# A written-out order for pooled attention and routed attention experts: another list of steps, PSUM banks and copy engines

## The chip, the core and the metric

The kernel runs on one core of a Trainium2 chip. A core has a matrix engine (TensorE, here PE), three elementwise engines (VectorE or DVE, ScalarE or ACT, GpSimd or POOL) and SyncE (SP), which here only issues stores. Each engine works through its own queue in order; engines wait for each other through semaphores. Matmul results go to PSUM, which has eight banks of 512 float32 columns in each of 128 partitions[...]. Times are microseconds (us) on the device; smaller is better.

## The reference

There are two parts. The first is attention with pooled keys and values: for each of 8 batches and 8 heads, 576 queries of 64 elements, and keys and values averaged over groups of 8 rows, so that 72 of each are left.

```python
k_p = k.reshape(B, H, Sp, pool, D).mean(axis=3)
v_p = v.reshape(B, H, Sp, pool, D).mean(axis=3)
scores = scale * np.matmul(q, k_p.transpose(0, 1, 3, 2))
attn = softmax(scores)                 # over the 72 pooled keys
x = np.matmul(attn, v_p)               # heads side by side: 576 x 512 per batch
```

The second takes that x. Four experts of width 64 each do causal attention over the 576 rows; a gate picks two experts for every row and weighs them.

```python
logits = x @ w_gate                    # top 2 of 4, softmax over the two
for e in range(E):
    q, k, v = x @ wq[e], x @ wk[e], x @ wv[e]
    a = softmax(causal(scale * q @ k.T))
    out += gate[e] * (a @ v @ wo[e])   # zero where e is not picked
```

## The kernel before

The work is cut into named steps, and a written-out list (`SEQ`, line 551) says in which order they are emitted. A token is a step, its arguments, the batch and, where it applies, the bank: `P_q1:0@7c` is the step P with arguments q and 1, of batch 0, into bank 7, cut into strips. The loop at line 642 reads the tokens one by one and calls the step's function. The framework turns data dependencies into semaphores; the order within PE, ACT, DVE and POOL is that of the list, and nothing else orders them. So a token's place in the list matters only against others of the same engine, and the relative place of tokens of two engines has no effect of its own.

**PE steps**, with their number over all batches:

- `PK`, `PV` (8 each) average k and v by a matmul with a constant matrix, into 32-column strips; `KT` (8) and `Q` (32) transpose the pooled k and the q.
- `E` (40) are the scores of two heads at once, each from 64 rows of the array; `E4` is the tail of 64 columns for all heads. `D` (24) sums the exponentials, `O` (40) multiplies them by pooled v, both in strips of 32 columns.
- `P` (40) projects x to the experts' q and k (`P_t` is the tail of 64 rows), `V` (36) to v and the gate's logits, in chunks of 128 rows.
- `S` (56) are the experts' scores, two experts at once from 64 rows each; `B` (36) multiplies their exponentials by v; `T` (24) transposes the result; `Y` (36) multiplies by wo.
- `H` are warm-up matmuls on zeros, 51 in all.

Three shapes of the array occur: whole (128 or 96 columns from over 64 rows), strips (32 columns) and half rows (64 rows). `PK`, `PV`, `D` and `O` are always in strips, `E` and `S` always in half rows. A trailing `c` on a token (`cut`, line 179) makes `wide` (line 187) cut a whole matmul into four strips of 32 columns with the same result.

**Reading steps** have small letters: each takes its PE step's bank out to SBUF. `e` and `s` (exponentials), `d` (logarithm of the sums) and `x` (exponential of its negative) are always ACT's; `o` and the normalisation `bz`, `bg`, `b` always DVE's; so are nine of the ten gate steps `g`. For `kc`, `kt`, `vc`, `r` (transposed q), `p`, `v`, `t` and `y` (the result), a trailing `d` chooses DVE, none ACT. `c0` to `c4` put the weights in order.

**POOL** issues every load: `L_q0:3` is the first of six loads of q for batch 3, `L_k` and `L_v` have three each, `W0` to `W4` load the weights, converting float32 to bfloat16 as they go. There are three raw buffers each for q, k and v (`NRAW`, line 55), so a load of batch b waits until batch b - 3 has been used. Between the loads POOL does the causal masks `a` (`am`, line 442): one instruction for each diagonal block of 128, two blocks for the tiles 1 and 2.

**Stores** are issued by SP as soon as a `y` is done (`z`, line 536); the last ones partly by ACT. Y4 of the last batch is cut into two halves of 256 columns in two banks, `ya` and `yb`.

Of the kernel before, what the change touches and what calls it, by code (L numbers as in the profile page):

```python
# [21 lines left out]
def kernel(  # L22
# [152 lines left out]
    def copy(dve, out, in_):  # L175
        (nc.vector.tensor_copy if dve else nc.scalar.copy)(out=out, in_=in_)  # L176
# [334 lines left out]
    def Y(b, bank, c):  # L511
        p0 = 128 * place(b, c)
        last = (b, c) == (B - 1, 4)
        for n0 in (0, 256) if last else (0,):
            n = 256 if last else 512
            for ep in range(NEP):
                wide(psum[:, bank ^ (n0 > 0), n0 : n0 + n],
                     oTs[2 * (b // 2 % 2) + ep][:, p0 : p0 + 128], wop[:, ep, n0 : n0 + n],
                     start=(ep == 0), stop=(ep == NEP - 1))

    def y(b, bank, dve, c, half=None, later=False):
        ofin = at[b, "ofin", c] if (b, "ofin", c) in at else ofp.tile([128, DM], FP32, name="ofin", tag="ofin")
# [13 lines left out]
    def z(b, c, queue):  # L536
# [15 lines left out]
        I:0 L_k0:0 L_k1:0 L_k2:0 J:0 K:0 H19:0@0 PK:0@0 kc:0 H4:0@1 KT:0@0 kt:0 L_q0:0 L_q1:0  # L552
        L_q2:0 L_q3:0 L_q4:0 L_q5:0 H8:0@1 Q2:0@0 r2:0 Q1:0@1 Q3:0@2 r1:0d r3:0 H1:0@3 E2:0@4
        e2:0 Q0:0@1 r0:0 E3:0@2 H5:0@0 E0:0@4 e3:0 L_v0:0 L_v1:0 E4:0@0 L_v2:0 PV:0@6 vc:0d e4:0
        e0:0 H2:0@2 D2:0@0 E1:0@2 O11:0@1 e1:0 H4:0@6 O01:0@2 O20:0@3 D1:0@4 d1:0 D0:0@5 x1:0
        M:0 L_k0:1 L_k1:1 L_k2:1 O10:0@6 O00:0@7 PK:1@4 d0:0 L_q0:1 o10:0 L_q1:1 L_q2:1 L_q3:1
        L_q4:1 kc:1d H3:0@5 KT:1@6 L_q5:1 H5:0@4 Q0:1@4 Q3:1@5 d2:0 x0:0 o01:0 o00:0 kt:1 o11:0
        x2:0 r0:1d W0:0 Q1:1@2 o20:0 W1:0 Q2:1@1 c0:0 E0:1@6 r3:1 r1:1d E3:1@4 c1:0d E1:1@2 e0:1
        c2:0d c3:0d P_q0:0@0 e3:1 W2:0 r2:1d W3:0 e1:1 P_t0:0@6 p_q0:0d p_t0:0d L_v0:1 P_k0:0@1
        S03:0@4 E4:1@6 E2:1@2 P_k1:0@0c c4:0d s03:0 L_v1:1 e4:1 V3:0@4c D2:1@5 D0:1@6 p_k1:0d  # L560
        p_k0:0d v3:0d P_q1:0@7c e2:1 D1:1@0 S00:0@2 d0:1 L_v2:1 d2:1 V1:0@6c p_q1:0d x0:1 s00:0
        V0:0@7c v0:0d PV:1@1 S01:0@2 S12:0@4 d1:1 V2:0@0c vc:1d x2:1 O20:1@1 v1:0d o20:1 s01:0
        O01:1@7 v2:0 L_k0:2 O11:1@6 x1:1 O00:1@2 L_k1:2 o01:1 o00:1 a03:0 O10:1@3 V4:1@0c o10:1
        o11:1 L_k2:2 s12:0 PK:2@1 P_t0:1@7 S02:0@4 kc:2 S10:0@2 g0:0 g1:0 v4:1 g2:0 KT:2@1
        L_q0:2 V3:1@6 V0:1@0 p_t0:1d s02:0 s10:0 g3:0 V2:1@7 kt:2d L_q1:2 L_q2:2 g4:0 L_q3:2
        L_q4:2 v3:1d L_q5:2 Q0:2@1 v2:1d Q3:2@6 v0:1 g5:0 r3:2d V1:1@2 Q1:2@0 Q2:2@3 r0:2 E0:2@6
        v1:1 E3:2@4 r1:2d a01:0 E1:2@0 e0:2 P_k0:1@2c g1:1 r2:2d P_q1:1@3c e1:2 g6:0 p_k0:1d
        e3:2 L_v0:2 L_v1:2 p_q1:1d D0:2@0 g0:1 L_v2:2 g7:0 g8:0 PV:2@1 vc:2d E2:2@6 d0:2 L_k0:3
        e2:2 E4:2@4 g2:1 P_q0:1@3c O00:2@2 L_k1:3 x0:2 O01:2@1 a00:0 O10:2@0 a10:0 L_k2:3 D1:2@6
        P_k1:1@7c e4:2 D2:2@4 d1:2 L_q0:3 x1:2 p_q0:1d d2:2 L_q1:3 a02:0 o01:2 O11:2@1 o00:2  # L570
        g3:1 PK:3@6 p_k1:1d L_q2:3 o11:2 S00:1@2 kc:3 S11:0@4 B01:0@7 L_q3:3 L_q4:3 o10:2 g4:1
        B00:0@6 g5:1 g6:1 g9:0 bz00:0 L_q5:3 KT:3@1 L_v0:3 P_q0:2@0 bz01:0 g7:1 kt:3d x2:2
        L_v1:3 g8:1 a12:0 g9:1 s11:0 L_v2:3 L_k0:4 p_q0:2d a11:0 V1:2@4 bg00:0 bg01:0 s00:1
        B10:0@5 v1:2 L_k1:4 S01:1@2 b00:0 S02:1@0 bz10:0 s01:1 L_k2:4 bg10:0 V0:2@4 L_q0:4
        L_q1:4 a01:1 B11:0@6 s02:1 b01:0 V3:2@7 Q1:3@2 v3:2 v0:2d Q2:3@4 b10:0 bz11:0 T0:0@5
        r1:3d S10:1@0 r2:3 bg11:0 E1:3@2 Q3:3@7 s10:1 b11:0 t0:0d r3:3d T1:0@6 Q0:3@5 P_k0:2@4
        S03:1@0 e1:3 t1:0d L_q2:4 L_q3:4 s03:1 L_q4:4 E3:3@6 r0:3d E4:3@2 e4:3 P_k1:2@5 L_q5:4
        p_k0:2d a00:1 p_k1:2d L_v0:4 E2:3@0 S12:1@2 PV:3@4 a03:1 e3:3 P_q1:2@5c vc:3d e2:3
        E0:3@0 s12:1 p_q1:2d W4:0 a02:1 L_v1:4 S11:1@6 B01:1@4 e0:3 bz01:1 bg01:1 B00:1@5 D1:3@2
        D2:3@3 O20:2@0 bz00:1 b01:1 o20:2 a12:1 s11:1 PK:4@1 D0:3@4 d1:3 d2:3 bg00:1 x1:3  # L580
        O00:3@6 L_v2:4 V2:2@0c O11:3@7 kc:4d O20:3@1 L_k0:5 b00:1 d0:3 o11:3 O10:3@3 v2:2 o10:3
        O01:3@2 Y3:0@5 a10:1 x0:3 P_t0:2@4 o01:3 Y1:0@0 x2:3 a11:1 o00:3 L_k1:5 B10:1@3 y3:0
        p_t0:2 Q0:4@2 y1:0 g1:2 o20:3 S01:2@4 S03:2@6 bz10:1 Y2:0@0c r0:4d s01:2 bg10:1 Y0:0@1c
        s03:2 PV:4@2 S02:2@4 b10:1 S12:2@6 y0:0d B11:1@3 g2:2 y2:0 vc:4d s02:2 Q1:4@0 Q2:4@1
        bz11:1 KT:4@2 Q3:4@4 T0:1@5 g3:2 r1:4d bg11:1 s12:2 kt:4d P_q0:3@0 b11:1 r3:4 r2:4d
        t0:1d E1:4@6 p_q0:3d e1:4 E3:4@2 E0:4@4 L_k2:5 P_k0:3@1 e3:4 T1:1@0 V2:3@6 P_q1:3@7
        E4:4@2 p_k0:3d g0:2 t1:1d g4:2 L_q0:5 L_q1:5 L_q2:5 v2:3d p_q1:3d e0:4 e4:4 S00:2@0
        E2:4@4 P_k1:3@6c e2:4 s00:2 Y3:1@7c L_q3:5 D0:4@2 L_q4:5 PK:5@3 D1:4@4 O11:4@5 y3:1d
        V1:3@7 p_k1:3d L_q5:5 d1:4 V0:3@0 Q3:5@4 kc:5 g5:2 L_v0:5 L_v1:5 v1:3d x1:4 KT:5@3 v0:3d
        Q0:5@7 P_t0:3@6 a12:2 Q1:5@0 r3:5d L_v2:5 d0:4 o11:4 r0:5d kt:5 Q2:5@1 S11:2@2 S10:2@4  # L590
        O00:4@7 p_t0:3 L_k0:6 x0:4 r1:5d O10:4@0 O01:4@6 L_k1:6 r2:5d s11:2 Y2:1@1c V4:3@2c
        o00:4 L_k2:6 L_q0:6 o01:4 s10:2 L_q1:6 a00:2 o10:4 D2:4@3 PV:5@7 Y0:1@6c y2:1 d2:4
        E4:5@4 vc:5 S00:3@0 L_q2:6 v4:3d y0:1d g6:2 a03:2 L_q3:6 L_q4:6 S02:3@2 x2:4 e4:5 V3:4@7
        g7:2 P_q0:4@6 L_q5:6 v3:4d s02:3 S10:3@4 p_q0:4d g8:2 s00:3 s10:3 S01:3@2 V3:3@7c L_v0:6
        v3:3d O20:4@6 P_k0:4@0c g1:3 o20:4 a11:2 s01:3 PK:6@1 p_k0:4d E1:5@4 g2:3 S11:3@6 e1:5
        E2:5@2 a01:2 a10:2 e2:5 P_k1:4@0 kc:6d g9:2 s11:3 B10:2@1 P_t0:4@4 Q3:6@5 V0:4@2 g3:3
        p_k1:4d L_v1:6 p_t0:4 bz10:2 L_v2:6 bg10:2 Y1:1@0 E3:5@6 a10:3 L_k0:7 g4:3 v0:4 r3:6d
        g0:3 E0:5@4 b10:2 y1:1 a02:2 S03:3@2 g5:3 B01:2@1 L_k1:7 B11:2@0 L_k2:7 s03:3 g6:3 a02:3
        B00:2@2 a00:3 g7:3 Q1:6@3 L_q0:7 e0:5 bz01:2 e3:5 KT:6@4 g8:3 g9:3 bz11:2 bg11:2 bg01:2
        V2:4@5 b11:2 L_q1:7 Q2:6@0 bz00:2 bg00:2 r1:6d b01:2 r2:6d D1:5@6 kt:6 D2:5@7 O10:5@4  # L600
        b00:2 a01:3 d1:5 d2:5 L_q2:7 v2:4d O01:5@3 x1:5 L_q3:7 x2:5 PV:6@1 D0:5@0 P_q1:4@7c
        O20:5@5 O00:5@2 vc:6d d0:5 a03:3 O11:5@6 x0:5 S12:3@0 o10:5 L_q4:7 T0:2@4 p_q1:4 a11:3
        o20:5 P_t0:5@5 o00:5 o01:5 s12:3 t0:2d p_t0:5 B01:3@7 B00:3@2 bz01:3 S02:4@0 o11:5
        L_q5:7 bg01:3 a12:3 bz00:3 s02:4 L_v0:7 E1:6@4 T1:2@3 B10:3@6 b01:3 V0:5@7 bg00:3 t1:2d
        bz10:3 V1:4@3 e1:6 bg10:3 v0:5 b00:3 S01:4@0 S00:4@4 b10:3 L_v1:7 Q0:6@2 v1:4d s01:4
        B11:3@6 Y0:2@3 P_k0:5@7 r0:6d bz11:3 E2:6@0 bg11:3 y0:2d S03:5@2 s00:4 b11:3 L_v2:7
        s03:5 E3:6@4 V1:5@6 p_k0:5d a02:4 T0:3@7 T1:3@2 v1:5d e2:6 e3:6 t0:3d Y1:2@3 P_q1:5@0
        S03:4@6 E0:6@4 t1:3d s03:4 y1:2d e0:6 g1:4 E4:6@2 e4:6 Y4:1@1c p_q1:5d a01:4 g2:4
        O11:6@6 D1:6@0 V2:5@7c D0:6@4 V3:5@5c D2:6@2 PK:7@3 y4:1d d1:6 g3:4 d2:6 x1:6 v3:5d kc:7
        O10:6@0 O01:6@1 g4:4 Y1:3@5c v2:5d o10:6 o11:6 P_k1:5@7c O00:6@0 d0:6 S10:4@2 y1:3  # L610
        p_k1:5d x0:6 S12:4@4 Q3:7@6 o01:6 s10:4 P_q0:5@7 KT:7@1 Q0:7@2 s12:4 V4:5@3 o00:6 kt:7
# [93 lines left out]
```

The softmax here doesn't subtract the row's maximum and nothing guards it: scores larger than these inputs give would overflow.

## Time and profile before

| | |
|---|---|
| median of 3 runs | 167.99 us |
| the runs | 167.83, 167.99, 222.52 us |
| span of the profiled execution | 165.0 us |
| its own time as a run | not given; the median is 3.0 us above the span |
| TensorE clock granted, mean | 0.996 |
| busy: PE, ACT, DVE, POOL | 157.0, 135.0, 123.8, 104.9 us |
| matmuls, and weight loads | 2463 each |
| last matmul starts, last copy ends | 160.37, 161.15 us |

A slice line of the page gives each engine's busy share in 40 equal slices of the span, in tenths; a timeline line gives start, length, engine, line, instruction, result and operands, shapes and count, and in brackets the idle time before it and what ended it. A group line gives, behind the bar, busy time and mean length. Matmuls overlap in the pipeline, so the time from one start to the next is what one costs. Most PE instructions have the line of the helpers `mm` (185) or `flip` (194) and most copies that of `copy` (176), so the tiles' names tell them apart: `qraw`, `kraw`, `vraw` are loads, `eta` the first part's exponentials, `xT` its transposed result, `qk` the experts' q and k, `etb` their exponentials, `vaug` their v, `osc` and `oT` the scaled result and its transpose, `ofin` the output.

### The profile page before, as it was taken

To read this page: it belongs to the slowest core of one execution; us is meant where nothing else is said; L and a number is where in the kernel's file an instruction comes from. 1 tells how busy PE (TensorE), PEld (TensorE's weight loads), DVE (VectorE), ACT (ScalarE), POOL (GpSimd) and SP (SyncE) were. 2 spreads that over 40 slices of the span, in tenths; PEclk is the share of its full clock that TensorE was granted. 3 is DMA by queue.
4 is the path that set the end of the run, shared out by engine and by line. 5 is a ranking of instruction groups with operands and counts; after the bars stand their busy time and mean duration, and the time that the engine had idled before them with its cause. 6 is when DMAs were issued, how large, how long until landed. Compare 5 with 4: busy or idle time off the path is not lost. (4 is left out here: it accounts for less than half of the span.)

```text
span 165.0 us, 6106 instructions
## 1 busy us (share of the span) xinstructions
PE 157.0 (95%) x2463; PEld 93.8 (57%) x2463; DVE 123.8 (75%) x410; ACT 135.0 (82%) x247; POOL 104.9 (64%) x178
## 2 busy tenths in 40 slices
PE   6999988999999999999999999999999999999980
PEld 2344354568557656654754878555647686555730
DVE  1101497589799859976988899998998989779960
ACT  3029758999998999888998997789997999898860
POOL 6999891899999999965959997400140211364100
PEclk9999999999999999999999999999999999999998
DMA  2999999999999999999999999923113043055875
GB/s 22 160 153 171 164 172 178 170 145 139 177 156 173 164 157 148 156 233 217 206 178 226 168 198 83 174 100 86 47 68 127 4 131 127 0 190 195 257 260 191
DMA packets 84204, 25.04 MB, mean 152 GB/s; under 512 B 79312, under 2 KB 79568, under 8 KB 84176
## 3 DMA queue, kind: packets, MB, share of 16 engines
q0 software_dynamic: 78928, 15.21, 110.6%
q1 hardware_dynamic: 5024, 9.05, 15.9%
q8 instruction: 19, 0.31, 0.7%
q10 hardware_dynamic: 224, 0.39, 0.6%
q14 instruction: 9, 0.07, 0.1%
HBM read 30.42 MB, written 9.44 MB: 242 GB/s over the span
## 5 line engine op out<-in xcount | busy, mean ns | idle before, releaser
L433 ACT ACTIVATE etb_97<-psum 128x1024 bf16<-128x1024 f32 x24 | 23.6, 1023 | 2.5 <-PE psum L185 2.4
L433 ACT ACTIVATE etb_98<-psum 128x1024 bf16<-128x1024 f32 x24 | 23.5, 1027 | 1.3 <-PE psum L185 1.1
L450 POOL TENSOR_SCALAR_AFFINE_SELECT etb_98<-etb_98 128x256 bf16<-128x256 bf16 x32 | 12.5, 410 | 17.4 <-ACT etb_98 L433 17.2
L450 POOL TENSOR_SCALAR_AFFINE_SELECT etb_97<-etb_97 128x256 bf16<-128x256 bf16 x32 | 12.4, 415 | 15.8 <-ACT etb_97 L433 15.7
L173 PE MATMUL psum<-warm 128*128 128x512 bf16 x51 | 15.2, 443 | 1.8 <-DVE onesd L146 1.3
L273 ACT ACTIVATE eta_91<-psum 96x1024 bf16<-96x1024 f32 x16 | 15.9, 1018 | 1.1 <-PE psum L185 1.1
L273 ACT ACTIVATE eta_92<-psum 96x1024 bf16<-96x1024 f32 x16 | 15.6, 1020 | 0.7 <-PE psum L185 0.6
L117 POOL DMA_DIRECT2D qraw_68<-in_q_dram x18 | 13.9, 775 | 1.2 <-PE psum L185 1.1
L176 DVE COPY ofin<-psum 128x512 f32<-128x512 f32 (+1 forms) x18 | 11.9, 673 | 3.2 <-PE psum L185 2.4
L117 POOL DMA_DIRECT2D qraw_69<-in_q_dram x18 | 13.8, 770 | 0.5 <-issue 0.5
L176 DVE CAST qk_99<-psum 128x512 bf16<-128x512 f32 (+1 forms) x16 | 10.5, 670 | 3.8 <-PE psum L185 3.6
L176 DVE CAST qk_100<-psum 128x512 bf16<-128x512 f32 (+1 forms) x16 | 10.5, 654 | 3.5 <-PE psum L185 3.5
L176 ACT COPY ofin<-psum 128x512 f32<-128x512 f32 (+1 forms) x19 | 10.7, 580 | 2.7 <-PE psum L185 1.8
L185 PE MATMUL psum<-wvg,xT_96 128*32 128x260 bf16 (+1 forms) x120 | 10.8, 275 | 0.0
L173 PEld LDWEIGHTS <-warm 128*128 128x128 bf16 x51 | 5.1, 111 | 9.5 <-issue 5.8
L185 PE MATMUL psum<-wvg,xT_95 128*32 128x260 bf16 (+1 forms) x156 | 10.5, 275 | 0.0
L185 PEld LDWEIGHTS <-etb_97 128*128 128x128 bf16 x240 | 8.8, 97 | 2.0 <-issue 0.4
L117 POOL DMA_DIRECT2D qraw_70<-in_q_dram x12 | 9.2, 784 | 0.0
L185 PEld LDWEIGHTS <-etb_98 128*128 128x128 bf16 x240 | 8.3, 97 | 1.4 <-issue 0.8
L185 PE MATMUL psum<-qk_100 64*128 64x64 bf16 (+4 forms) x96 | 8.8, 276 | 0.1
L117 POOL DMA_DIRECT2D kraw_71<-in_k_dram x9 | 7.0, 787 | 2.7 <-DMA qraw_70<-in_q_dram 1.8
L185 PE MATMUL psum<-qk_99 64*128 64x64 bf16 (+4 forms) x96 | 8.4, 277 | 0.0
(198 smaller groups left out, 452.8 us busy)
## 6 DMA issues: line engine op xcount, KB each, us to landing
out_dram<-ofin SPq DMA_DIRECT2D x31, 256.0 KB, 3.0
kraw_71<-in_k_dram POOLq DMA_DIRECT2D x9, 192.0 KB, 6.2
qraw_68<-in_q_dram POOLq DMA_DIRECT2D x18, 96.0 KB, 5.3
vraw_74<-in_v_dram POOLq DMA_DIRECT2D x9, 192.0 KB, 5.5
kraw_72<-in_k_dram POOLq DMA_DIRECT2D x9, 192.0 KB, 5.9
qraw_69<-in_q_dram POOLq DMA_DIRECT2D x18, 96.0 KB, 5.5
vraw_75<-in_v_dram POOLq DMA_DIRECT2D x9, 192.0 KB, 4.9
kraw_73<-in_k_dram POOLq DMA_DIRECT2D x6, 192.0 KB, 6.5
```

Of the source, the lines that this page charges most:

```text
L117: nc.gpsimd.dma_start(out=dst, in_=src)
L173: nc.tensor.matmul(out=psum[:, bank, :], lhsT=warm[:, 0:128], rhs=warm[:], start=True, stop=True)
L176: (nc.vector.tensor_copy if dve else nc.scalar.copy)(out=out, in_=in_)
L185: nc.tensor.matmul(out=out, lhsT=lhsT, rhs=rhs, start=start, stop=stop)
L273: nc.scalar.activation(out=eta[:, hp, :, 0:MAIN], in_=psum[0:KR, bank : bank + 2, :], func=EXP, scale=ATT_EXP_SCALE,)
L433: nc.scalar.activation(out=et[:, ep, :, eo : eo + n], in_=psum[:, bank : bank + 2, 0:n], func=EXP, scale=MOE_EXP_SCALE,)
L450: nc.gpsimd.affine_select(out=blk, in_=blk, pattern=[[0, 2], [1, 128]], compare_op=ISGE, fill=0.0, base=0, channel_multiplier=-1,)
```

## The change

All tokens but a few stay; their order, banks and engines are new. The number of steps of each kind is the same. Against the list before:

- 50 steps have the strip mark `c`, where 34 had it: V 23 (11), P 20 (14), Y 7 (9).
- The warm-ups are 44 (51): 15, 5 and 6 before the first Q steps, where 19, 4 and 8 stood.
- ACT has 17 p (8), 23 y (18), 17 v (14), 6 t (3), 3 r (8), 2 kc (5), no c (1); DVE has the others.
- The loads of one tensor no longer come in the order of their chunks, loads of later batches come ahead of those of earlier ones, and the masks `a` stand between other loads than before.
- The last steps are Y3 and Y2 of batch 7, each copied whole; before, the last was Y4. `z2:7`, a store issued by ACT, is gone.
- The second half of Y4 of batch 7 goes to the next bank (`bank + half`) instead of the one with the last bit flipped, since its bank is now 5.

The diff, cut to the lines of code and to those stretches of the list that the prediction speaks of:

```diff
-                wide(psum[:, bank ^ (n0 > 0), n0 : n0 + n],
+                wide(psum[:, bank + (n0 > 0), n0 : n0 + n],
...
-            copy(half == 1, ofin[:, cols], psum[:, bank ^ half, cols])
+            copy(half == 1, ofin[:, cols], psum[:, bank + half, cols])
...
-        I:0 L_k0:0 L_k1:0 L_k2:0 J:0 K:0 H19:0@0 PK:0@0 kc:0 H4:0@1 KT:0@0 kt:0 L_q0:0 L_q1:0
-        L_q2:0 L_q3:0 L_q4:0 L_q5:0 H8:0@1 Q2:0@0 r2:0 Q1:0@1 Q3:0@2 r1:0d r3:0 H1:0@3 E2:0@4
...
-        L_q4:1 kc:1d H3:0@5 KT:1@6 L_q5:1 H5:0@4 Q0:1@4 Q3:1@5 d2:0 x0:0 o01:0 o00:0 kt:1 o11:0
-        x2:0 r0:1d W0:0 Q1:1@2 o20:0 W1:0 Q2:1@1 c0:0 E0:1@6 r3:1 r1:1d E3:1@4 c1:0d E1:1@2 e0:1
-        c2:0d c3:0d P_q0:0@0 e3:1 W2:0 r2:1d W3:0 e1:1 P_t0:0@6 p_q0:0d p_t0:0d L_v0:1 P_k0:0@1
...
-        p_k0:2d a00:1 p_k1:2d L_v0:4 E2:3@0 S12:1@2 PV:3@4 a03:1 e3:3 P_q1:2@5c vc:3d e2:3
-        E0:3@0 s12:1 p_q1:2d W4:0 a02:1 L_v1:4 S11:1@6 B01:1@4 e0:3 bz01:1 bg01:1 B00:1@5 D1:3@2
...
-        O00:3@6 L_v2:4 V2:2@0c O11:3@7 kc:4d O20:3@1 L_k0:5 b00:1 d0:3 o11:3 O10:3@3 v2:2 o10:3
-        O01:3@2 Y3:0@5 a10:1 x0:3 P_t0:2@4 o01:3 Y1:0@0 x2:3 a11:1 o00:3 L_k1:5 B10:1@3 y3:0
...
-        bz02:7 Y2:7@1 bg02:7 bg12:7 y3:7 b02:7 y2:7p Y0:7@0 z2:7 y0:7 Y1:7@2 b12:7 T12:7@4
-        t12:7d y1:7 t12:6d T02:7@6 t02:7d Y4:7@6 ya4:7 yb4:7d
+        I:0 L_k2:0 J:0 L_k1:0 L_q4:0 L_k0:0 L_q0:0 L_q2:0 L_q3:0 L_q1:0 L_q5:0 K:0 L_v2:0 L_v0:0
+        H15:0@7 PK:0@0 kc:0d H5:0@7 KT:0@2 H6:0@7 Q0:0@6 kt:0 M:0 L_v1:0 L_q0:1 Q3:0@2 r0:0d Q1:0@3
...
+        KT:1@6 L_q5:1 x1:0 H7:0@5 Q2:1@2 kt:1 o01:0 o11:0 o10:0 r2:1d x2:0 Q1:1@7 o20:0 W0:0 c1:0d
+        Q3:1@5 c0:0d Q0:1@6 r0:1d W1:0 W3:0 r1:1 E2:1@1 e2:1 E1:1@3 e1:1 P_q1:0@7 r3:1d E3:1@5 e3:1
+        L_v0:1 E0:1@0 c3:0d c2:0d W2:0 e0:1 p_q1:0d P_k1:0@2c P_t0:0@7c p_k1:0d L_v1:1 D1:1@5 d1:1
...
+        p_k0:1 a02:0 E0:2@0 L_k1:4 a12:0 e2:2 Q1:2@7 L_q3:5 r1:2d P_q1:1@2 p_q1:1d P_q0:1@5 E1:2@6
...
+        L_q1:5 g9:1 B11:0@0 bz11:0 B01:0@5 bz01:0 S01:1@3 E3:3@1 L_v1:3 bg01:0 a11:1 bg11:0 s01:1
+        b10:0 b11:0 b01:0 P_k0:2@6 V3:2@7 L_v0:4 e3:3 Q3:4@0 a10:1 V2:2@3 p_k0:2d E2:3@4 r3:4d v3:2
+        e2:3 L_q5:5 E4:3@1 a00:1 v2:2d e4:3 S03:2@6 L_v2:4 s03:2 D0:3@0 P_q0:2@3c p_q0:2d D1:3@4
+        L_q4:6 V1:2@5c PK:4@1 v1:2d S02:2@2 kc:4d Q0:4@6 r0:4d T0:0@5 t0:0d Q1:4@7 d0:3 KT:4@1 x0:3
+        s02:2 L_q4:5 d1:3 Q2:4@0 r2:4d a01:1 T1:0@6 kt:4 t1:0d a12:1 x1:3 D2:3@2 PV:3@5 vc:3d L_v1:4
+        d2:3 S01:2@3 E2:4@0 e2:4 L_q2:5 r1:4d a02:1 B01:1@6 bz01:1 bg01:1 b01:1 L_k1:5 W4:0 a03:1
+        B10:1@2 B00:1@7 E3:4@0 L_v1:6 O00:3@5 s01:2 bz10:1 bg10:1 P_k1:2@6c a01:2 L_k0:5 L_k2:5
...
+        B01:7@3 bg11:7 y0:7 b11:7 bz01:7 T12:7@0 t12:7 T02:7@2 t02:7d Y1:7@1 y1:7 bg01:7 b01:7
+        Y4:7@5 T11:7@0 ya4:7 T01:7@3 t01:7 yb4:7d t11:7d Y3:7@6 y3:7 Y2:7@0 y2:7
```

## The prediction, made before the run

> **What bounds the kernel now.** I read, in this order, the busy shares and the 40 slices of the page, the windows by stage, the engines' timelines at the start, in the middle and at the end, and the table of instruction groups. The page, and then the windows (columns: stretch, length, busy us and count of PE, weight loads, DVE, ACT, POOL; clock, DMA share, GB/s):
>
> ```profile
> PE 157.0 (95%) x2463; PEld 93.8 (57%) x2463; DVE 123.8 (75%) x410; ACT 135.0 (82%) x247; POOL 104.9 (64%) x178
> ...
> PE   6999988999999999999999999999999999999980
> ...
> POOL 6999891899999999965959997400140211364100
> ```
> ```profile
> 0.00:26.20 26.20, 23.49 (x195) 10.20 (x195) 8.67 (x30) 13.30 (x22) 23.76 (x35) 1.00 1.71 142
> 26.20:105.00 78.80, 78.75 (x1432) 49.94 (x1431) 65.94 (x205) 72.98 (x137) 68.17 (x110) 1.00 1.79 171
> 105.00:150.00 45.00, 44.92 (x699) 27.59 (x697) 39.71 (x128) 40.36 (x74) 11.04 (x29) 1.00 0.35 102
> 150.00:160.70 10.70, 9.84 (x146) 6.12 (x143) 9.03 (x49) 8.17 (x17) 1.95 (x5) 1.00 0.65 225
> ```
>
> PE is the bound from 26.2 to 160.7 us. Its busy time overstates that, since matmuls overlap, so I laid the PE's start times beside the order list. A 512-column matmul is followed by the next 0.216 us later, a 65-column one 0.030, a 260-column one 0.111. Priced so, all matmuls but the warm-ups come to 129.2 us. Of the 134.4 us between the first projection (P_q0:0 at 26.23) and the last matmul's end (160.64), 130.1 are such matmuls and changes of tile shape; 4.3 us are real waits, 0.95 of them before B10:1 at 65.98 and 3.36 after it. Before 26.2 the PE waits for loads and for ACT and spends 13.6 us on warm-ups. POOL is nearly solid until 105 us: it issues all loads and does the causal masks between them.
>
> Three timelines carry the prices. The first is PE, a change from half-row tiles (64*96) to column strips (128*32); the second POOL; the third POOL and ACT at the start:
>
> ```profile
> 41.13 0.38 PE L185 MATMUL psum<-qT_86,kpT_79 64*96 64x512 bf16 x2
> 41.35 0.38 PE L185 MATMUL psum<-qT_84,kpT_79 64*96 64x512 bf16 x2
> 41.66 0.40 PE L185 MATMUL psum<-xT_95,wkp_122 128*32 128x512 bf16 x4
> ```
> ```profile
> 48.00 0.77 POOL L450 TENSOR_SCALAR_AFFINE_SELECT etb_97<-etb_97 128x256 bf16<-128x256 bf16 x2
> 48.71 0.77 POOL L117 DMA_DIRECT2D vraw_74<-in_v_dram  x1
> 49.47 0.77 POOL L117 DMA_DIRECT2D kraw_72<-in_k_dram  x1
> ```
> ```profile
> 17.48 0.78 POOL L117 DMA_DIRECT2D qraw_69<-in_q_dram  x1 [0.47 <-issue]
> 18.25 0.90 POOL L130 DMA_DIRECT2D wst_q<-in_moe_wq_dram  x1
> ...
> 24.46 0.62 ACT L176 COPY wqp_120<-wst_q 128x512 bf16<-128x512 bf16 x1 [1.18 <-DMA wst_q<-in_moe_wq_dram]
> ```
>
> The reader sees that a pair of half-row matmuls takes 0.22 us when its like follows and 0.31 when the shape changes, so a change costs 0.09 to 0.10 (0.096 over all); that one mask block takes 0.357 us of POOL (0.71 for two) and one load 0.762; and that the first projection can't come before wq lands at 24.46.
>
> **What the Trainium skill says.** "TensorEngine Tiling (Array Packing)", Key Properties: changing the tiling mode drains TensorE. The trace agrees: 0.096 us each. The same page, Feature Incompatibilities: column tiling excludes the fast weight load. Here it shows no cost: a 128x32 load takes 96 ns, a 128x128 one 97, and P_k0:1 in sixteen strips holds PE from 41.66 to 42.53, as long as P_q0:0 in four whole matmuls from 26.23. "Perfetto Trace Analysis", Summary of the profiler window per engine type: a software-issued DMA's slice ends when its descriptors are generated, not when data moved. The trace agrees: 0.77 us on POOL, 4.9 to 6.9 us to landing. "TensorE: Matmul & The Clock Gate", Part 1: the clock is halved again after an idle window of about 3.4 us. The trace has only the first part of it: early warm-ups start 0.43 us apart, later ones 0.216.
>
> **The change part by part.** The sum is made on the profiled execution's span, 165.0 us; the median of the runs shown, 167.99, stands 3.0 above it, and I add that at the end.
>
> *Tiles.* Strip-cut steps go from 34 to 50 (V 11 to 23, P 14 to 20, Y 9 to 7): 2463 matmuls become 2804. Four 260-column strips take 0.115 us against 0.111; 12 V steps of four such groups cost 12 x 4 x 0.004 = 0.2. The 341 more weight loads lie under streaming matmuls; were that cover gone, 341 x 0.096 = 33 us would show, but at present strips as dense as these are hidden. I take 0.2.
>
> *Order on PE.* Counted in the lists, changes of tile shape go from 97 to 104, and from 80 to 92 after the first projection: 12 x 0.096 = 1.15 us, all on the path. With one more E step (0.22) and two single warm-ups (0.43) behind that point, the PE work from the first projection to the end is 131.9 instead of 130.1: +1.8, the shape changes included.
>
> *Start.* The first 21 loads keep their total, so q of batch 1 and then wq reach POOL as late as now (18.25). k of batch 0 is no longer complete after three loads but after four and the iota: 0.76 + 0.25 = 1.0 us later, under the wait for q (landed at 12.2 now). Three r and one kc leave ACT, and the wq copy goes to DVE. So the first projection goes as soon as wq is copied: 24.46 + 0.66 (the DVE copy of wqp_121) = 25.1, instead of 26.23: a gain of 1.1 at most; if batch 1's q-transposes or exponentials are later than that, nothing. I take the 1.1.
>
> *Copy engines.* ACT takes 9 more p, 5 more y, 3 more v and 3 more t, and gives up 5 r, 3 kc and a c. By start-to-start times (512-column copy 0.478 on ACT, 0.608 on DVE; 576 bf16 0.536 on ACT, 0.368 on DVE) ACT's total goes from 126.4 to 130.1, DVE's from 109.7 to 103.3. ACT has idle time, but in the stretches of 10 us of PE work its load peaks at 10.9 us (now 10.8), so part of the 3.7 will reach the PE. Between 0 and 3.7, I take 0.5 (an estimate from these loads).
>
> *POOL's queue.* This is the step that decides. The loads for batches 4 to 6 are moved ahead of batch 1's masks. In the new list 68 loads, 5 weight loads and 22 mask blocks end with a03:1: 68 x 0.762 + 5 x 0.82 + 22 x 0.357 + 0.25 (iota) = 64.0, from 1.3 on, plus the 1.0 that POOL has lost by 24 us now (0.47 at 17.48 is half of it): 66.3, seen by PE at 66.4. The step B10:1, the first half of batch 1's attention-times-v, reads that mask's block. PE reaches it at 25.1 + 38.84 of work + 0.95 of waits as now = 64.9. So it waits about 1.5 us, and everything behind it on PE with it. In the present list a03:1 stands behind ten loads fewer, B10:1 lies as far behind the first projection (38.80 of PE work), and PE runs through there without a wait. Buffers don't hold POOL up: each moved load's buffer was freed over 1 us before POOL reaches it. Of the other loads the closest are q of batch 4, v of 4 and k of 6; with the landing times above each arrives as PE does, after the stall with 2 us to spare.
>
> *End.* Now the last step is Y4:7, copied in two halves by ACT and DVE and stored on two queues; then the last two are Y3:7 and Y2:7, both copied whole by ACT one after the other, and stored on SP. The second copy starts 0.478 after the first and takes 0.59, against 0.42 for a half:
>
> ```profile
> 160.73 0.42 DVE L176 COPY ofin<-psum 128x256 f32<-128x256 f32 x1 [0.76 <-ACT ofin L176]
> 161.22 0.47 SPq L540 DMA_DIRECT2D out_dram<-ofin  x1
> 161.24 0.54 ACTq L540 DMA_DIRECT2D out_dram<-ofin  x1
> ```
> Last matmul's end to the end of the span is 4.4 us now; I take 4.9. The changed bank of Y4:7's second half (bank 6, not 7) costs nothing: its reader has long left it.
>
> **Sum:** 66.4 (B10:1 starts) + 93.06 (PE work from there) + 3.36 (waits as now) + 0.2 + 0.5 + 4.9 = 168.4; with the 3.0, **171.4**, 2.0% above 167.99.
>
> **Rivals.**
> *POOL is in time.* Then B10:1 doesn't stall: 168.4 - 1.5 - 0.5 = 166.4, or 169.4. For it: POOL's gaps need not recur, and 1 us less lag leaves 0.5 of stall. Against: the sum of its work alone ends at 65.3.
> *The new order waits in many places.* The waits double, from 4.3 to 8.6: 172.7, or 175.7. For it: of 477 returns to a PSUM bank, those with under 1 us to spare beyond the copy go from 167 to 179, ACT is fuller, and with 44 warm-ups instead of 51 the PE stands idle for 2 us before the first k lands, where a halved clock would cost the startup 2 to 4 us. Against: the returns under 0.5 us are fewer (23 for 27), and masks and v stand further ahead of their users.
> *Not slower:* the waits go. T to Y distances are at least 1.2 us beyond the copy (now 0.4), v to B 8.9 (now 3.5); if the 4.3 us of waits halve and POOL's lag stays under 0.2, the end is 25.1 + 131.9 + 2.2 + 4.9 = 164.1, or 167.1. It decides once waits stay under 3 us. More can't be had: the wq landing and 131.9 us of PE work stand.
>
> **Numbers.** The forecast has 0.38, POOL in time 0.21, many waits 0.33, not slower 0.08. 2% of this kernel (3.4 us) is about what a measurement can tell from no change. The forecast lies on that line, and as a wait is likelier missed than imagined, 0.22 of its 0.38 go beyond it; many waits lies beyond it (0.33); the rest is within it, but for 0.03 of the last case, which would need nearly every wait gone: faster 0.03, same 0.42, slower 0.55. The range reaches from 168.4, below the second case, to 176.5, beyond the third; it leaves out the last case and the worst of the third.
>
> **What would show it.** A PE gap before B10:1 released by POOL's mask; the first projection at 25 us; ACT busy some 3 us more; PE waits after 66 us near 3.4; about 104 shape changes; 4.9 us after the last matmul. Wrong if POOL has idle gaps before 66 us, if the early PE clock drops, or if a load lands late.

## The result, and the profile after

The changed kernel takes 171.54 us (median of 4 runs, 170.80 to 173.02), the kernel before 167.91. The ratio is 1.027, with a 95% interval from 1.020 to 1.034; one run of the kernel before, of 222.52 us, was a slow one and is left out of it. The forecast was 171.4 in a range from 168.4 to 176.5. The number was met by luck: three of the steps behind it were missed, and errors of both signs met in the sum. The profiled execution took 171.84 us, with a span of 170.1. In every execution listed the time stands 1.7 to 1.9 us above its span, so the span of 165.0 before belonged to an execution of about 166.7, a quick one.

The page of the kernel after, to be held against the lines at the head of the prediction:

```profile
PE 156.2 (92%) x2787; PEld 94.6 (56%) x2804; DVE 118.6 (70%) x396; ACT 139.0 (82%) x261; POOL 105.1 (62%) x178
...
PE   7679899888999999899999999999999999999960
...
POOL 7999886878999999999994085301002253214300
PEclk9969999999999999999999999999999999999996
...
q8 instruction: 22, 0.36, 0.9%
```

PE is busy for less time than before in a longer span: it waits more. DVE gave up 5 us and ACT took 4. In slice 3 the granted clock is down to 0.6, after the idle stretch ahead of the first k; this sets the start back, as shown further down. The last line is a DMA queue that the prediction passed over: 22 packets, 0.36 MB, of instructions. (Of 2804 matmuls 17 have no record; where instructions are counted below, the list fills them in.)

What the PE waited for after (waits of PE: total, times, longest):

```profile
PE psum L185 <- DMA kraw<-in_k_dram: 2.6, 2, 2.3
...
PE psum L185 <- issue: 1.2, 3, 0.9
...
PE psum L194 <- issue: 0.6, 1, 0.6
PE psum L185 <- POOL etb L442: 0.6, 1, 0.6
PE psum L185 <- ACT oT L176: 0.6, 1, 0.6
```

And where, in PE's timeline of the kernel after:

```profile
32.48 1.24 PE L185 MATMUL psum<-xT,wqp 128*32 128x512 bf16 x13
34.58 0.39 PE L185 MATMUL psum<-xT,wqp 128*32 128x512 bf16 x2 [0.86 <-issue]
...
40.09 0.62 PE L194 MATMUL psum<-ident,qraw 96*128 96x96 bf16 x9
41.33 0.54 PE L194 MATMUL psum<-ident,qraw 96*128 96x96 bf16 x9 [0.61 <-issue]
...
67.70 0.72 PE L185 MATMUL psum<-vaug,etb 128*128 128x65 bf16 x18
69.03 1.02 PE L185 MATMUL psum<-vaug,etb 128*128 128x65 bf16 x28 [0.61 <-POOL etb L442]
```

The last pair is the predicted wait of B10:1 for batch 1's mask; it comes after the first four matmuls of the step, which start at 68.14. The two pairs above it are not in the prediction. The PE stops in the middle of a step, P_q0:0 and Q2:2, whose first part has already run with the same inputs, and the profile finds no semaphore that ends the stop ("issue").

Laid against the order list as in the prediction (matmuls by their spacing, 0.096 us for a change of shape), the span grew by 5.1 us like this: first projection 26.09 for 26.23, -0.1; PE work from there 131.9 for 130.1, +1.8; the two stops 1.47 and 0.76, +2.2; the mask 0.78; all other waits -0.4; from the last matmul's end to the end of the span 5.2 for 4.4, +0.8. These are two single executions; by the ratio the change costs 4.6 us, by the two medians 3.6.

### The profile page after: what moved, and what is told of

Read it like the earlier page. It is cut to its first block, busy times and chain, and to the rows that moved or that the text cites. A ratio compares the mean times of both kernels' runs of the same rounds, so it can differ in the third digit from the quotient of the medians.

```text
span 170.1 us, 6728 instructions
## 1 busy us (share of the span) xinstructions
PE 156.2 (92%) x2787; PEld 94.6 (56%) x2804; DVE 118.6 (70%) x396; ACT 139.0 (82%) x261; POOL 105.1 (62%) x178
## 4 chain that ended last, share of the span: by engine, by line
PE 56%; POOL 19%; DMA 11%; ACT 5%; issue 4%; DVE 1%; ACTq 0%; POOLq 0%
PE psum L185 47%; DMA kraw<-in_k_dram 8%; POOL qraw L117 7%; PE psum L194 5%; POOL etb L450 5%; PE psum L173 4%; DMA qraw<-in_q_dram 3%; ACT eta L273 3%; POOL vraw L117 3%; POOL kraw L117 3%; POOL etb L442 1%; ACT etb L433 1%; DVE osc L489 1%; ACT etb L427 1%; ACT oT L176 0%
## 5 line engine op out<-in xcount | busy, mean ns | idle before, releaser
L433 ACT ACTIVATE etb<-psum 128x1024 bf16<-128x1024 f32 x48 | 48.7, 1038 | 3.5 <-PE psum L185 3.2
L450 POOL TENSOR_SCALAR_AFFINE_SELECT etb<-etb 128x256 bf16<-128x256 bf16 x64 | 24.9, 411 | 39.3 <-ACT etb L433 32.9
L117 POOL DMA_DIRECT2D qraw<-in_q_dram x48 | 36.9, 775 | 2.9 <-issue 1.4
L273 ACT ACTIVATE eta<-psum 96x1024 bf16<-96x1024 f32 x32 | 31.8, 1032 | 2.6 <-PE psum L185 2.5
L317 DVE TENSOR_TENSOR xT<-psum,rza 128x512 bf16<-128x512 f32 x32 | 21.0, 684 | 9.6 <-PE psum L185 4.9
L185 PE MATMUL psum<-wvg,xT 128*32 128x260 bf16 (+1 forms) x420 | 22.2, 275 | 0.0
L185 PE MATMUL psum<-xT,wqp 128*32 128x64 bf16 (+3 forms) x306 | 20.2, 282 | 1.1 <-issue 1.0
L185 PE MATMUL psum<-xT,wkp 128*32 128x512 bf16 (+3 forms) x328 | 19.8, 290 | 0.2
L185 PE MATMUL psum<-vaug,etb 128*128 128x65 bf16 x480 | 19.1, 193 | 0.8 <-POOL etb L442 0.6
L185 PE MATMUL psum<-wop,oT 128*32 128x512 bf16 (+2 forms) x108 | 18.9, 376 | 0.8 <-ACT oT L176 0.6
```

The lines of the kernel that those rows point to most:

```text
L117: nc.gpsimd.dma_start(out=dst, in_=src)
L185: nc.tensor.matmul(out=out, lhsT=lhsT, rhs=rhs, start=start, stop=stop)
L273: nc.scalar.activation(out=eta[:, hp, :, 0:MAIN], in_=psum[0:KR, bank : bank + 2, :], func=EXP, scale=ATT_EXP_SCALE,)
L317: nc.vector.tensor_tensor(out=xT[:, 2 * g + t, mcols(b)], in0=psum[:, bank, :], in1=rz[:, g, 0:MAIN], op=MULT)
L433: nc.scalar.activation(out=et[:, ep, :, eo : eo + n], in_=psum[:, bank : bank + 2, 0:n], func=EXP, scale=MOE_EXP_SCALE,)
L450: nc.gpsimd.affine_select(out=blk, in_=blk, pattern=[[0, 2], [1, 128]], compare_op=ISGE, fill=0.0, base=0, channel_multiplier=-1,)
```

## The experiments

Each was timed beside the kernel before, whose median was 167.43, 167.56 and 167.16 us in the three groups of four. Where it isn't said otherwise, an edit is made to the changed kernel.

### Stops of the PE: fewer instructions

```diff
-P_t0:0@7c ... P_k0:0@6c ... V0:0@6c ... P_q0:0@1c V2:0@2c V3:0@6c V1:0@2c P_t0:1@4c
+P_t0:0@7 ... P_k0:0@6 ... V0:0@6 ... P_q0:0@1 V2:0@2 V3:0@6 V1:0@2 P_t0:1@4
```

> Eight strip-cut steps of the stretch from 29 to 46 us (P_k0, P_t0, P_q0, V0 to V3 of batch 0 and P_t0 of batch 1) become whole tiles. That adds 10 changes of tile shape (0.96 us of PE work by the price of the prediction) and takes away 168 matmuls with as many weight loads. Theory 'instructions': the PE stops at 33.34 and at 40.52 us, 1.57 and 0.76 us beyond its work, because the next 16 KB of its own instructions (256 of them) have not come through the loaded DMA engines; with fewer instructions in that stretch both stops go, 2.3 us, and the time falls by 1.4: about 170.1. Rival 'data': the stops are late loads or late copies, and stay; the added changes of shape make it 172.5. Third possibility: the shape changes cost 1.0 and one stop of two goes, 171.5.

170.25 us, ratio 1.018 (1.012 to 1.023). Both stops are gone: laid against the list, the PE has lost 0.59 us between the first projection and PK:3, where the changed kernel has lost 2.76. The gain was had although the PE work rose to 132.9. The time alone would not settle it, since the intervals of the two ratios overlap; the missing stops do. But the PE now comes sooner to B10:1, and in PE's timeline of this kernel the wait for the mask has grown from 0.78 to 1.36:

```profile
66.27 0.72 PE L185 MATMUL psum<-vaug,etb 128*128 128x65 bf16 x18
68.18 1.00 PE L185 MATMUL psum<-vaug,etb 128*128 128x65 bf16 x27 [1.19 <-POOL etb L442]
```

### The same cause, put into the kernel before

```diff
-P_q0:0@0 ... P_t0:0@6 ... P_k0:0@1
+P_q0:0@0c ... P_t0:0@6c ... P_k0:0@1c
```

> The kernel before with one thing changed: its first three projections (P_q0, P_t0 and P_k0 of batch 0) are cut in strips. They stand side by side, between half-row steps, so the number of changes of tile shape is the same and the PE work on the matmuls is the same; there are 72 matmuls and 72 weight loads more. Theory 'instructions': the PE's own instructions come in 16-KB blocks of 256, and 144 more of them in 3 us let it run out of them as in the changed kernel: a stop in which the PE waits for nothing in the profile at or shortly after 30 us, 0.5 to 2 us in sum, and a time 0.5 to 2 us above before. The prediction's step ('the more weight loads lie under streaming matmuls') and the rival that the stops come from the order of the loads: no stop, and before's time within 0.3 us.

169.97 us, ratio 1.014 (1.010 to 1.019): 2.4 us for strips that change neither the sum of the PE's work nor its changes of shape, and no order at all. PE's timeline of this kernel:

```profile
31.07 0.39 PE L185 MATMUL psum<-xT,wqp 128*32 128x512 bf16 x2
33.28 1.04 PE L185 MATMUL psum<-xT,wqp 128*32 128x512 bf16 x14 [1.82 <-issue]
```

It is one stop, in P_q1:0, a step that was in strips already and wasn't touched. Count the PE's instructions from the start of the program, a weight load and a matmul one each. This stop is ahead of number 702. So is the first stop of the changed kernel, and its second is ahead of number 958, exactly 256 later. With 16 KB a packet, 256 instructions are 64 bytes each.

### More warm-ups at the start

```diff
-H15:0@7 PK:0@0
+H26:0@7 PK:0@0
```

> 26 warm-up matmuls for 15 ahead of the first pooling step: the PE no longer stands idle for 2.3 us before k lands at 9.5. Theory 'clock': the halved clock from 10 to 14 us (5 warm-ups in 2.1 us instead of 1.1) is what took the gain of 1.1 us that the prediction gave to the start; Q0:0 starts at 12.3 instead of 14.23, the first projection at 25.1 instead of 26.09, and the time is 170.5. Rival 'weights': the first projection waits for wq, which lands at 25.15 here (issued at 18.05, 7.1 us of flight for 6.2 before), and for two copies on DVE behind it; it moves by 0.3 us at most, and the time is 171.2 to 171.5.

171.31 us, ratio 1.024 (1.019 to 1.029), no difference that can be told from the changed kernel. The clock stayed up, and the first projection came at 26.05 all the same, after wq had landed at 25.67: 'weights' holds for this execution. It doesn't clear the clock (see the start, in the section on the prediction), since in the changed kernel's own profile it isn't wq that the first projection waits for. The run decides something else. Eleven matmuls more stand ahead of everything, and the stop has moved by eleven matmuls, from behind the 14th strip of P_q0:0 to behind the 3rd, and is still ahead of instruction 702:

```profile
32.68 0.40 PE L185 MATMUL psum<-xT,wqp 128*32 128x512 bf16 x3
33.54 1.02 PE L185 MATMUL psum<-xT,wqp 128*32 128x512 bf16 x13 [0.46 <-issue]
```

So the stop belongs to the number of the instruction and not to the step: no load, copy or bank can be its cause. The DMA records give the start of each instruction packet, and with it this table (us):

| kernel | PE stops ahead of | packet starts | PE goes on | between |
|---|---|---|---|---|
| changed | 702 in P_q0:0 | 32.19 | 34.58 | 2.39 |
| changed | 958 in Q2:2 | 38.89 | 41.33 | 2.44 |
| e11_cut_before | 702 in P_q1:0 | 30.83 | 33.28 | 2.45 |
| e1_warm | 702 in P_q0:0 | 31.23 | 33.54 | 2.30 |
| e10_masks | 702 in P_q0:0 | 31.54 | 33.78 | 2.24 |
| e10_masks | 958 in Q2:2 | 37.77 | 40.25 | 2.48 |
| e2_kfirst | 702 in P_q0:0 | 31.19 | 33.57 | 2.38 |
| e2_kfirst | 958 in Q0:2 | 37.64 | 40.04 | 2.40 |
| before (no stop) | 702 | 30.86 | 34.32 | 3.46 |
| e8_whole (no stop) | 702 | 32.04 | 39.27 | 7.23 |

In all kernels run there are sixteen such stops of 0.45 us or more. Each is ahead of instruction 702 or a multiple of 256 behind it (958, 1470, 2494), and each ends 2.2 to 2.5 us after its packet's start; where the PE gets to the block later than that, nothing is lost. "Runtime: NRT & Kernel Launch", Instruction fetch mechanics, has the frame: instructions come in 16-KB blocks of 256 over a DMA queue of their own, the next block while the current one runs. The packets agree. The page also says that the slow issue of instructions hides this; here it doesn't, and the measurement decides. The packet of a block seems to be asked for when the PE goes into the block ahead: in the changed kernel it starts within 0.9 us of that from 112 us on, when the loads are over, but 2.2 to 4.3 us after it at 20 to 42 us, when POOL's loads hold the DMA engines. With 2.4 us more, the PE then can't run through 256 instructions, 128 matmuls, in less than 6.0 to 6.7 us (3.6 and 4.3 at its two stops). Strips bring four times as many instructions for the same work: instructions 446 to 701 of the changed kernel took the PE 4.8 us.

### Half the bytes of k and v

```diff
-            dst = raw[b % NRAW][:, c, :, :, :].rearrange("p h t d -> p h (t d)")
-            src = T[b, :, 2 * KR * c : 2 * KR * (c + 1), :].rearrange("h (p t) d -> p h (t d)", t=2)
+            dst = raw[b % NRAW][:, c, :, 0, :]
+            src = T[b, :, 2 * KR * c : 2 * KR * c + KR, :].rearrange("h p d -> p h d")
...
-                mm(psum[32 * c : 32 * c + 32, bank, :], mat[:, :], raw[:, c, :, t, :],
+                mm(psum[32 * c : 32 * c + 32, bank, :], mat[:, :], raw[:, c, :, 0, :],
```

> Each load of k and v brings one row of two, so it has as many descriptors (768) as now but half the bytes (96 KB for 192), and both pooling matmuls read that one row: half of k and v is left out of the computation. POOL issues the same loads in the same order. Theory 'bytes': POOL waits 0.3 to 0.8 us ten times between 25 and 46 us because the DMA engines are behind with the bytes of loads issued before, and the PE's instructions come late for the same reason. Then those waits fall under 1 us in sum, the last mask of batch 1 ends near 66.3 instead of 68.9, the stops at 33.3 and 40.5 us go, and the time is 168.0 to 169.5. Rival 'descriptors': POOL waits by the number of loads under way, not by their bytes; POOL is as late as now and the time is within 0.5 us of 171.5.

167.09 us, ratio 0.999 (0.997 to 1.002): 'bytes', and more than it asked for. POOL's waits between 24 and 47 us, first of the changed kernel, then of this one (total, times, longest):

```profile
POOL qraw L117 <- issue: 1.2, 2, 0.6
POOL kraw L117 <- DMA wst_k<-in_moe_wk_dram: 0.8, 1, 0.8
POOL qraw L117 <- DMA wst_q<-in_moe_wq_dram: 0.6, 1, 0.6
POOL qraw L117 <- PE psum L185: 0.6, 1, 0.6
POOL vraw L117 <- DMA kraw<-in_k_dram: 0.4, 1, 0.4
POOL qraw L117 <- DMA vraw<-in_v_dram: 0.3, 1, 0.3
```

```profile
POOL qraw L117 <- issue: 0.3, 1, 0.3
POOL kraw L117 <- DMA wst_k<-in_moe_wk_dram: 0.3, 1, 0.3
```

POOL's gaps in that stretch go from 3.9 to 0.6 us, and a03:1 ends at 65.1 instead of 69.0, near the 66.3 of the prediction's sum. So POOL wasn't late by its own work: loads of k and v issued back to back carry more than the DMA engines, which move 172 GB/s between 20 and 45 us of the changed kernel, bring away (192 KB every 0.762 us, the price of one load, would be 258 GB/s), and POOL has to wait with the next one. The stop at 702 shrinks to 0.7 us and that at 958 is gone: their packets start 2.7 and 2.2 us after the PE has gone into the block ahead, where it was 3.6 and 4.3; k lands earlier, the first projection comes at 23.96, and B10:1 doesn't wait.

### The masks ahead of the loads

```diff
-... L_v0:3 L_q1:5 L_v1:3 a11:1 L_v0:4 a10:1 L_q5:5 a00:1 L_v2:4 L_q4:6 L_q4:5 a01:1 a12:1 L_v1:4 L_q2:5 a02:1 L_k1:5 W4:0 a03:1
+... L_v0:3 L_v1:3 a11:1 L_v0:4 a10:1 a00:1 L_v2:4 a01:1 a12:1 L_v1:4 a02:1 W4:0 a03:1 L_q1:5 L_q5:5 L_q4:6 L_q4:5 L_q2:5 L_k1:5
...
-... L_k1:6 a03:3 a11:3 a00:3 L_k2:7 a12:3 a02:3 L_v0:7 L_k0:7
+... L_k1:6 L_k2:7 L_k0:7 L_v0:7 a03:3 a11:3 a00:3 a12:3 a02:3
```

> On POOL alone: batch 1's masks stand ahead of six loads for batches 5 and 6 (q1, q5, q4, q2 and k1 of 5, q4 of 6) that now stand among them, and the last loads for batch 7 (two of k, one of v) ahead of the mask a03:3 that POOL now waits for from 91 to 98 us. All else is the changed kernel. Theory 'POOL late': the wait of 0.78 us ahead of B10:1 at 68.14 goes, and so does that of 0.5 us for k of batch 7 at 110: 171.5 - 1.3 = 170.2. Rival 'something else is late there': the PE has waited 2.3 us before, and whatever else is late (a copy of ACT, v for the step) takes the place of the mask: 171.0 to 171.5.

171.21 us, ratio 1.022 (1.017 to 1.026). Both waits named are gone, as the first theory says, yet the time hardly moved, as the rival says. What took their place is in part the edit's own. The late masks keep their order on POOL, but in the written list they came to stand further behind the steps of the other engines: a02:6, ahead of B10:6 in the changed kernel, stands behind B02:6 here. It waits 9.7 us for the PE, where it didn't wait in the changed kernel (the longest such wait there is 5.1), and the PE then loses 0.9 us ahead of Y3:5 and Y0:6, at 154 to 157. So the place of a token against those of other engines did have an effect, other than the description of the list says; that the semaphores are derived from the list's order would explain it, but no run here shows how. The stop at 702 stayed (1.8 us), that at 958 too (0.5), and one at 1470, three blocks on, cost 0.9.

### Both

The edits of the first and of the last kernel together.

> The changed kernel with the eight strip-cut steps of e8_whole as whole tiles and POOL's order of e10_masks. Theory: the two losses are separate. e8_whole lost its stops at instructions 702 and 958 but then waited 1.36 us for the mask ahead of B10:1, since the PE came there sooner; e10_masks had no wait for the mask, but its stop at 702 stayed. With both, neither is left: e8_whole's 170.25 less 1.3 is 168.9, a ratio of 1.009 to before. Rival: another wait takes the mask's place again, as in e10_masks, and it stays at 170.0 to 170.5.

169.83 us, ratio 1.016 (1.014 to 1.018): by the ratios 0.3 us less than e8_whole, where 1.3 was expected. In the profile neither the mask's wait nor the stops at 702 and 958 are left; a stop of 0.5 has come at 2494, and what is lost ahead of Y3:5 and Y0:6 (0.9) is the same as in e10_masks. So this pair doesn't separate cleanly, and the price of the mask's wait alone stays open within 0.3 to 1.4 us. The PE's work alone is 2.8 us more than before here (132.9 for 130.1), and 1.6% are 2.7 us.

### Tiles of the kernel before in the new order

```diff
-P_q1:0@7 ... P_t0:0@7c P_k0:0@6c ... P_q0:0@1c (44 steps)
+P_q1:0@7c ... P_t0:0@7 P_k0:0@6 ... P_q0:0@1 (44 steps)
```

> The changed kernel with the cut of every projection, v and output step as in the kernel before: 44 steps differ. Orders, banks and copy engines stay. The number of changes of tile shape goes from 104 to 160 (92 to 148 after the first projection), since the strips were chosen to fit the order of the PE; the number of matmuls goes from 2804 to 2456. Theory: a change of shape costs 0.096 us, so the PE's work goes from 131.9 to 137.3 (+5.4), and the stops at instructions 702 and 958 (2.2 us) go with 348 matmuls fewer: 171.5 + 5.4 - 2.2 = 174.7. Rival: a change of shape is hidden where the PE waits anyway: 170 to 172.

174.62 us, ratio 1.046 (1.043 to 1.048), for 174.7 expected. 56 changes of shape more at 0.096 us, less the two stops, which the trace doesn't have. The price of a change of shape holds, and the strips do fit the order: they save 5.4 us of changes and lose 2.2 by their number. That the time fits to a tenth is chance, though: in the profile the mask's wait is 1.5 us again, and the first projection comes at 25.07, 1.0 us sooner than in the changed kernel's.

### Copy engines of the kernel before in the new order

```diff
-kc:0d ... r0:0d ... kc:1 ... c0:0d ... r1:1 ... v0:0 p_q0:0 (73 copies)
+kc:0 ... r0:0 ... kc:1d ... c0:0 ... r1:1d ... v0:0d p_q0:0d (73 copies)
```

> The changed kernel with each copy on the engine that it has in the kernel before (57 copies differ; 63 of them on ACT instead of 74). Theory: ACT's 4 us more of work cost the PE nearly nothing in the changed kernel: the trace has no wait of the PE for a copy on ACT but the one at the end (0.75 us), so with the old engines the time is within 1 us of 171.5, more if copies now meet on one engine that were spread for this order. Rival 'ACT is the bound': the time falls by 2 us or more, under 169.5.

196.12 us, ratio 1.174 (1.170 to 1.178). Neither theory. (73 copies differ, 42 of them now on DVE and 31 on ACT; the 57 above is a miscount.) ACT is 1.1 us less busy than in the changed kernel and DVE 4.5 us more, but the PE now meets one copy after the other (waits of PE, of this kernel):

```profile
PE psum L185 <- DVE osc L489: 3.1, 5, 1.1
...
PE psum L185 <- DVE qk L176: 2.1, 2, 1.4
PE psum L185 <- ACT vp L176: 1.7, 1, 1.7
PE psum L185 <- DVE xT L317: 1.7, 4, 0.6
PE psum L185 <- ACT L L176: 1.6, 3, 0.7
```

The sum of an engine's copies says little about their price: which engine stands free where the order has a copy decides, and 73 choices made for another order cost 24.6 us.

### POOL's order of the kernel before

```diff
-I:0 L_k2:0 J:0 L_k1:0 L_q4:0 L_k0:0 ...  (all L, W and a tokens)
+I:0 L_k0:0 L_k1:0 L_k2:0 J:0 L_q0:0 ...  (in the order of the list before)
```

> The changed kernel with the loads and masks of POOL in the order of the kernel before (one mask, a02:7, moved to the end, since its scores come later in this order of the PE); the orders of the other engines, banks, tiles and copies are the changed kernel's. Theory 'POOL's order': POOL again pauses some 4 us at 25 for the first mask, the DMA engines catch up, the PE's stop at instruction 702 shrinks from 1.5 to under 0.8, the waits for the mask (0.78) and for k of batch 7 (0.56) go: 169.3. Rival 'the orders belong together': the PE asks for q of batch 2 all at once and for v in another order, and loads that come in before's order are late: 171 or more, with waits for DMA in the PE's list.

192.38 us, ratio 1.143 (1.137 to 1.150): the rival, 21 us beyond the 171 that it named. Masks that come before loads in the old list wait for scores that come late in the new one, and the loads behind them wait along. POOL's timeline of this kernel:

```profile
57.34 1.53 POOL L117 DMA_DIRECT2D qraw<-in_q_dram  x2
63.80 0.41 POOL L450 TENSOR_SCALAR_AFFINE_SELECT etb<-etb 128x256 bf16<-128x256 bf16 x1 [4.93 <-ACT etb L433]
64.30 3.05 POOL L117 DMA_DIRECT2D qraw<-in_q_dram  x4
```

The PE waits 11.8 us for q in all. In these waits the granted clock falls to half as well, three times and for 20.5 us together (from 48.8, 69.3 and 113.7 us on), so part of the loss is matmuls at half the clock. The stop at 702 was there too (1.4 us).

### The end

```diff
-Y4:7@5 T11:7@0 ya4:7 T01:7@3 t01:7 yb4:7d t11:7d Y3:7@6 y3:7 Y2:7@0 y2:7
+Y4:7@5 T11:7@0 T01:7@3 t01:7 t11:7d ya4:7 yb4:7d Y3:7@4 y3:7 Y2:7@0 y2:7d
```

> The changed kernel with another end: the copies t01:7 and t11:7 (one on ACT, one on DVE) stand ahead of the halves of Y4:7, Y3:7 goes to bank 4 (its bank 6 holds Y4:7's second half), and the last copy, of Y2:7, is DVE's. Theory 'copy order': the PE's wait of 0.75 us ahead of Y3:7 goes, and from the last matmul's end to the end of the span it is 4.5 instead of 5.1 us: 1.2 us less, 170.3 where the changed kernel has 171.5. Rival: the output stores, not the copies, set the end, and the halves of Y4:7 that now come later are stored later: within 0.4 us of 171.5.

171.41 us, ratio 1.024 (1.020 to 1.028). The rival: the wait ahead of Y3:7 is 0.63 for 0.75, and the last matmul's end stands 5.1 us ahead of the end of the span, where it was 5.2 in the changed kernel.

### k first

```diff
-I:0 L_k2:0 J:0 L_k1:0 L_q4:0 L_k0:0 L_q0:0 ... H15:0@7
+I:0 L_k0:0 L_k1:0 L_k2:0 J:0 L_q4:0 L_q0:0 ... H20:0@7
```

> The changed kernel with the three loads of k for batch 0 first again, as in the kernel before, and 20 warm-ups for 15 ahead of the first pooling step. Theory 'bytes at the start': loads of k carry twice the bytes of loads of q, so with k first the DMA engines are busy sooner, what is issued by 18 us has landed sooner, wq lands at 24.5 instead of 25.1, the first projection starts at 25.4 instead of 26.09, and the time is 0.7 us less, 170.8. Rival: the DMA engines are filled by 5 us in either order and wq lands where it did; the first projection and the time stay within 0.3 us of the changed kernel's.

171.24 us, ratio 1.025 (1.022 to 1.028): no difference that can be told. In its profile the first projection comes at 24.98, but among the six profiles with the changed kernel's own start it comes anywhere from 25.07 to 26.13, and at 25.07 and 25.12 in the two of them in which the clock stayed up, as it did here. So one profile doesn't decide, and k first shows nothing that the clock doesn't.

### One part of the change alone, in the kernel before

```diff
-c0:0 E0:1@6 r3:1 r1:1d E3:1@4 c1:0d
+E0:1@6 r3:1 r1:1d E3:1@4 c0:0d c1:0d
```

> The kernel before with one thing of the change: the first copy of the weights (wqp_120) moves from ACT to DVE, just ahead of its sister there. On ACT it waits 1.18 us for wq to land and holds the q-transpose's copy qT_90 behind it, and through it E3:1 and the first projection. Theory: qT_90 is copied at 24.1 instead of 24.98, the first projection starts at 25.4 instead of 26.23, and the time is 0.8 us less, 166.6. Rival: DVE has its own queue there, wqp_121 and the copies of wk come 0.3 us later, and the PE meets that or a late k-projection at once: within 0.3 us of before.

166.56 us in 22 runs, ratio 0.995 (0.993 to 0.997): 0.9 us less than before, and the fastest of all versions here that leave nothing out. The PE's wait of 0.7 us for qT_90 isn't in its list any more. Its profiled execution was its slowest (167.87): the PE waited 1.2 us for a load of v there, so it doesn't show the start at its new time, and the gain rests on the times alone.

## Why the prediction was right, and where it wasn't

*The sum.* It had B10:1 run from 66.4, with the mask there, and its masked part ran from 69.03: 2.6 short (1.0 from the start and 2.2 from the stops, less 0.7 of the mask's wait). From there it had 102.0 us to the end of the span, and there were 101.1. It added 3.0 for what lies around the span, which is 1.7 in every execution. 2.6 less 0.9 less 1.3 is the 0.4 by which the profiled 171.84 stands above 171.4. The number was met because errors cancel, which is luck.

*Tiles: the step that failed.* "The 341 more weight loads lie under streaming matmuls ... I take 0.2." The loads do lie there; their fetch doesn't. 2.2 us of stops in the profiled execution, shown by three programs that stop at one instruction number in three different places of two steps, by the 1.3 us won with fewer instructions and by the 2.4 us lost with more in the kernel before.

*Order on PE:* +1.8 by 0.096 for a change of shape. Right: the price is what a change costs in e5_tiles too, where 56 more of them made the PE's work 5.4 us longer.

*Start: the second step that failed.* A gain of 1.1 expected, 0.1 measured. Two things were late. wq landed at 25.1 instead of 24.46 (7.1 us after its issue, 6.2 before). And the clock fell to half for 3.4 us from 9.8 us on; the prediction had named that, but given it nothing in the sum. Of the six profiles with this start the clock stayed up in two (e10_masks, e5_tiles): there Q0:0 starts at 12.7 us, E1:1, the step ahead of the first projection, at 24.5 to 24.6, and the first projection at 25.12 and 25.07, as forecast. In the other four, the changed kernel's among them, Q0:0 starts at 13.9 to 14.3, E1:1 at 25.4 to 25.8, and the first projection at 25.73 to 26.13, in two of them (e8_whole, e13_both) although wq had landed by 24.5. PE's timelines, of the changed kernel and then of e10_masks, show the difference. In each the first line ends with E1:1 and the second is the first projection. In the changed kernel it follows E1:1 without a wait, since the copy of wq that it reads was done at 25.78; in e10_masks it waits for that copy.

```profile
25.45 0.70 PE L185 MATMUL psum<-qT,kpT 64*96 64x512 bf16 x4
26.09 1.04 PE L185 MATMUL psum<-xT,wqp 128*128 128x512 bf16 x4
```

```profile
24.25 0.70 PE L185 MATMUL psum<-qT,kpT 64*96 64x512 bf16 x4
25.12 1.04 PE L185 MATMUL psum<-xT,wqp 128*128 128x512 bf16 x4 [0.17 <-DVE wqp L176]
```

e1_warm can't show this, since wq landed late in its profile. How much of this reaches the end is open: the three runs of e5_tiles with a mean clock of 0.979 took 174.56 to 175.28 us, the three with 0.997 or 0.998 took 174.07 to 174.68, and in e1_warm's time no gain can be told.

*Copy engines:* 0.5 on the path. ACT's busy time rose by 4.0 and DVE's fell by 5.2, where 3.7 and 6.4 had been worked out; no wait of the PE for a copy on ACT but the one at the end shows in the profile. That the rest was taken as nothing was right for these choices; the way of costing them by sums wasn't (e4_copy).

*POOL's queue:* the mechanism was right, the place, B10:1, too. The term that was mis-sized is the lag: 1.0 was carried over from the kernel before, and it was 3.7, because loads without masks between them wait for the DMA engines (e9_half). In the kernel before, POOL loses 4 us in that stretch as well, but in one wait for the scores of the mask a03:0 (3.8 us), while the DMA engines catch up, and its a03:1 has ten loads fewer ahead of it. The wait came to 0.78 instead of 1.5 only because the PE was late itself; without the stops it is 1.36 (e8_whole) and 1.5 (e5_tiles).

*End:* 4.9 from the last matmul's end. 5.2 in the profiled execution, and 4.4 to 5.3 over the eight profiles with this end, 4.9 in the mean. Right.

*Rivals.* "Waits in many places" holds in part: PE waits after the first projection went from 4.3 to 7.0 us, for a reason that it didn't have; the halved clock that it named did come. "POOL in time" is excluded for the changed kernel.

## What to carry to other kernels

An instruction costs the engine its fetch, too: where a loop of strips or small matmuls replaces a few large ones, divide the instructions by the time in which they are to run, and see whether a block of 256 is used up sooner than it comes while loads hold the DMA engines. A stop "<- issue" in the middle of a step whose inputs are there is to be counted out in instruction numbers before it is put down to data. Order, copy engines and the order of loads were chosen together, so putting one of them back alone measures the mismatch, not the part; a part that can be put into the other kernel alone, such as one copy, tells more.

## What the runs showed of the hardware that was not expected

- PE instructions come in packets of 16 KB, 256 instructions. From the start of a packet to the first instruction out of it there were 2.2 to 2.5 us in sixteen stops; in the changed kernel the packet starts up to 4.3 us after the PE has gone into the block ahead when loads hold the DMA engines, within 0.9 us when they don't.
- POOL's issue of loads runs into the DMA engines: 3.9 us of gaps in 23 us with 192 KB in each load of k and v, 0.6 with 96 KB in as many descriptors.
- The granted clock fell to half after an idle stretch of 2.3 us of the PE (7.2 to 9.5 us; five warm-ups took 2.1 us then). The length of the stretch alone doesn't decide: of the six profiles with this start it fell in the four with 1.9 to 2.3 us of idle PE and stayed up in the two with 3.2. So the idle window of about 3.4 us that the prediction cites isn't what these profiles show. The time didn't change by what could be told when the stretch was filled.
